# Retention, routed experts and channel mix on one core: the int64 narrowing's steps laid out one a call, with a third buffer for their results

## The chip, the core and the metric

The kernel runs on one core of a Trainium2 chip. The metric is the device time of one execution in microseconds (us); lower is better. The text names the engines as the profile does: PE (TensorE, matmuls), PEld (its weight loads), DVE (VectorE), ACT (ScalarE), POOL (GpSimd), SP (SyncE, which here only issues DMAs). Each engine works through its own instructions strictly in the order in which the program gives them. A piece of work waits for its inputs and for the buffer that it writes, and everything behind it on that engine waits as well.

## The reference

Three stages follow one another; the second and third are what the change touches.

```
B, H, S, D = 2, 8, 768, 64           # retention with decay, block by block -> out [B, H, S, D]
x = out.transpose(0, 2, 1, 3).reshape(2, 768, 512)

# experts: E = 8, F = 1024; every token goes to one expert e (argmax, or the one before, by a local gate)
h = np.maximum(x[b, s] @ w1[e], 0.0)           # w1 [8, 512, 1024]
out[b, s] = p[e] * (h @ w2[e])                 # w2 [8, 1024, 512]

# channel mix
xk = mu_k * x + (1.0 - mu_k) * x_prev;  xr = mu_r * x + (1.0 - mu_r) * x_prev
k = np.maximum(xk @ w_k, 0.0);  v = k * k @ w_v
r = 1.0 / (1.0 + np.exp(-(xr @ w_r)));  return r * v
```

The inputs `w_k` [512, 1024], `w_v` [1024, 512] and `w_r` [512, 512] of the last stage reach the kernel as 64-bit floats, viewed as int64, and have to be narrowed to 32 bits on the chip.

## The kernel before

**Matmuls by split values.** Every f32 operand is held as a high part (rounded for the fast matmul form) and a low part (the rest), and `split3` (L652) makes three matmuls of each product: high by high, high by low, low by high. Each weight therefore passes through `w_split` (L144): ACT copies a loaded piece of 128x1024 f32 to the high tile (L155), DVE subtracts to get the low one (L156), and a new load of a piece, four ahead, is put on SP's queue (L140, pool `stp`, 4 buffers `raw`). An expert has 8 such pieces, 4 of `w1` and 4 of `w2`.

**The expert loop** (L953). For each of 8 experts, `up` computes four pieces of h: 24 matmuls each into one of three PSUM buffers `ps_h`, then ACT makes `hh` (L669) and DVE makes `hl` (L670), which frees the buffer. `flip` transposes the next expert's inputs (PE L649) and splits them (ACT L173, DVE L174). `down` computes two pieces of y from the four `hh`/`hl`, 24 matmuls of 512 columns each. After expert 1's `up` and `flip`, `weights` (L807) computes softmax weights once: small DVE and ACT work.

**Side work.** After each piece of `up` (four times) and twice in each half of `down` (four times) the loop calls `side_w` (L932). The calls are counted through the kernel, c = 0 to 63; c mod 8 = 0 to 3 lie in `up`, 4 to 7 in `down`. A call does `ws` splits of weight pieces, then `ns` steps of the narrowing, then `vs` conversions of narrowed rows that stay on the chip (`divide`); the three numbers are set in L937 to L943. Splits run about one expert ahead of their use: the splits in `up(e)` are for the second weight of expert e + 1, those in `down(e)` for the first of expert e + 2.

**Narrowing** (`narrow`, L754) is a generator that goes on by one step each time `next(conv)` is called. After a first step that puts two reads of int64 pieces on SP's queue (`raw64`, 512 KB each, 2 buffers, L767), 20 pieces of 128x512 values follow, each in three steps:

- first step: `narrow_1` (L743, L744), two DVE instructions on t1, which holds the magnitude that ACT has made from the int64 piece (L739, `begin`);
- second step: `narrow_2` (L747, L748), which writes t2;
- third step: `narrow_3` (L751, L752), after which t2 holds the f32 values. The step then puts `begin` of the next piece on ACT (its magnitude) and the read of the piece after that on SP, which takes over the buffer just used up.

18 of the 20 results are written to DRAM from t2 (L788, 256 KB each), by SP in the call after; the last two stay in t2 until `divide`. The last 9 of the 73 weight pieces are loads of these written values, in calls 48 to 56. t1 and t2 are tags of the pool `tp` with 2 buffers each, and `mix_pair` (L889) uses the same tags in the channel mix.

Of the kernel before, what the change touches and what calls it, by code (L numbers as in the profile page):

```python
# [10 lines left out]
F32 = mybir.dt.float32  # L11
# [3 lines left out]
I32 = mybir.dt.int32  # L15
# [6 lines left out]
P = 128  # L22
# [22 lines left out]
def kernel(  # L45
# [84 lines left out]
    for kind, i, src, n, f in plan:  # L130
        m = PIECE // f
# [12 lines left out]
    def w_split(k=1, eng=dve):  # L144
        for _ in range(k):
            if at[1] >= len(pieces):
                return
            while at[0] <= at[1]:
                w_load()
            kind, i, src, n, f, j, m = pieces[at[1]]  # L150
            if (kind, i) not in W:
                W[kind, i] = w_tiles(kind, i, n, f)
            hi, lo = W[kind, i]
            t = staged.pop(at[1])
            act.copy(out=hi[:, j : j + m, :], in_=t)  # L155
            eng.tensor_tensor(out=lo[:, j : j + m, :], in0=t, in1=hi[:, j : j + m, :].bitcast(F32), op=ALU.subtract)  # L156
            at[1] += 1
            w_load()
# [469 lines left out]
    tp = ctx.enter_context(tc.tile_pool(name="tp", bufs=2))  # L628
# [4 lines left out]
    with ExitStack() as bctx:  # L633
# [104 lines left out]
        def magnitude(raw, t):  # L738
            act.activation(out=t.bitcast(F32), in_=words(raw)[2], func=AF.Abs)  # L739

        def narrow_1(t):

            dve.tensor_scalar(out=t.bitcast(F32), in0=t.bitcast(F32), scalar1=2.0**-15, scalar2=TOP64, op0=ALU.max, op1=ALU.min)  # L743
            dve.tensor_scalar(out=t, in0=t, scalar1=3, scalar2=0x3FFFFFFF, op0=ALU.logical_shift_left, op1=ALU.bitwise_and)  # L744

        def narrow_2(raw, t, t2, p2):
            dve.scalar_tensor_tensor(out=t2, in0=words(raw)[1], scalar=-(1 << 30), in1=t, op0=ALU.bitwise_and, op1=ALU.bitwise_or)  # L747
            dve.tensor_scalar(out=p2, in0=t2, scalar1=-(1 << 23), scalar2=None, op0=ALU.bitwise_and)  # L748

        def narrow_3(raw, p2, low, t2, x):  # L750
            dve.scalar_tensor_tensor(out=low, in0=words(raw)[0], scalar=2.0**-52, in1=p2, op0=ALU.mult, op1=ALU.mult)  # L751
            dve.tensor_tensor(out=x, in0=low, in1=t2.bitcast(F32), op=ALU.add)  # L752

        def narrow():  # L754

            n = DM
            parts = []
            for src, dst in ((wk, wk32), (wr, wr32), (wv, wv32)):
                sv, dv = (x.rearrange("p a b -> p (a b)") for x in (src, dst))
                parts += [(sv[:, j : j + n], dv[:, j : j + n]) for j in range(0, dv.shape[1], n)]  # L760
            parts += [(wv[:, j, :], j) for j in range(NV, NF)]
            raws, ts = {}, {}

            def read(k):
                if k < len(parts):
                    raws[k] = bp.tile([P, n], mybir.dt.int64, name=f"raw64_{k}", tag="raw64")
                    sp.dma_start(out=raws[k], in_=parts[k][0])  # L767

            def begin(k):
                if k < len(parts):  # L770
                    ts[k] = tp.tile([P, n], I32, name="t1", tag="t1")
                    magnitude(raws[k], ts[k])

            read(0)
            read(1)
            yield
            begin(0)
            for k in range(len(parts)):
                t2 = tp.tile([P, n], I32, name="t2", tag="t2")
                narrow_1(ts[k])  # L780
                yield
                narrow_2(raws[k], ts[k], t2, ts[k])
                yield
                narrow_3(raws[k], ts[k].bitcast(F32), ts[k].bitcast(F32), t2, t2.bitcast(F32))
                if isinstance(parts[k][1], int):
                    whole.append((parts[k][1], t2.bitcast(F32)))
                else:
                    written.append(lambda t=t2, k=k: sp.dma_start(out=parts[k][1], in_=t.bitcast(F32)))  # L788
                begin(k + 1)
                read(k + 2)  # L790
                yield
# [3 lines left out]
        def divide():  # L795

            j, x = whole.pop(0)
            hi, lo = (w[:, j, :] for w in W["w2", NE])
            act.copy(out=hi, in_=x)
            dve.tensor_tensor(out=lo, in0=x, in1=hi.bitcast(F32), op=ALU.subtract)  # L800

        conv = narrow()
        perm = bp.tile([P, 2, 2 * P], F32R, name="perm", bufs=1)
        ylast = []
# [83 lines left out]

        def mix_pair(i, a, hi, lo, old, new, quick=False):  # L889

            t, m = (tp.tile([P, 2, 2 * P], F32, name=x, tag=x) for x in ("t1", "t2"))
            r = slice(2 * a, 2 * a + 2)

            def older(j):
                x, m1 = old(j), mus1[:, i, 2 * a + j : 2 * a + j + 1]
                o = t[:, j, 2 * P - x.shape[-1] :]
                if not j and x.shape[-1] < 2 * P:
                    (dve if quick else pool).memset(t[:, :, 0:1], 0.0)
                if quick:
                    dve.tensor_scalar(out=o, in0=x, scalar1=m1, scalar2=None, op0=ALU.mult)  # L900
                else:
                    act.activation(out=o, in_=x, func=AF.Copy, scale=m1)

            def newer(j):
                d = 2 * a + j
                dve.scalar_tensor_tensor(out=m[:, j, :], in0=new(j), scalar=mus[:, i, d : d + 1], in1=t[:, j, :], op0=ALU.mult, op1=ALU.add)
                if quick:
                    act.copy(out=hi[:, d, :], in_=m[:, j, :])

            for f in (older, newer):  # L910
                for j in range(2):
                    f(j)
            if not quick:
                act.copy(out=hi[:, r, :], in_=m)
            dve.tensor_tensor(out=lo[:, r, :], in0=m, in1=hi[:, r, :].bitcast(F32), op=ALU.subtract)

        def mix_first(a, i=0):
            if not a:
                x0[i] = mix_tiles(i, 0)
            mix_pair(i, a, *x0[i], lambda j: px[1 + a][:, j, 0 : 2 * P - 1], lambda j: px[1 + a][:, j, :], not i)  # L920
# [11 lines left out]
        def side_w():  # L932
            c = calls[0]
            calls[0] += 1
            late = list(written)

            ws, ns, vs = 1, 1, 0  # L937
            if c < 4:
                ws, ns = (2, 2, 1, 1)[c], c == 2
            elif c < 24:  # L940
                ns = 2 if c % 8 in (4, 6) or c in (5, 7, 13, 15) else 1
            elif c >= 52:
                ws, ns, vs = ((1, 2, 0), (1, 0, 0), (1, 0, 0), (1, 0, 0), (1, 0, 0), (1, 0, 1), (1, 0, 0), (0, 0, 1), (1, 0, 0), (1, 0, 0), (0, 0, 0), (0, 0, 0))[c - 52]  # L943
            w_split(ws)
            for _ in range(ns):
                next(conv, None)
            for _ in range(vs):
                divide()
            for w in late:
                w()  # L950
            del written[: len(late)]

        for e in range(NE):  # L953
            up(e, side_w)
            if e + 1 < NE:
                flip(e + 1)
            if e + 2 < NE:
                gather(e + 2, gidx, NT)
            if e == 1:
                weights()  # L960
            if e == 3:
                weights_by_slot()
            down(e, side_w)
# [3 lines left out]
    with ExitStack() as mctx:  # L967
# [48 lines left out]
        def mix(n, i):  # L1016
            if n >= NN:
                return None
            x = mix_tiles(i, n)
            for a in range(2):  # L1020
                mix_pair(i, a, *x, lambda j: xt[n][:, 2 * a + j, 0:GS], lambda j: xt[n][:, 2 * a + j, 1 : 1 + GS])
            return x
# [164 lines left out]
```

## Time and profile before

| what | us |
|---|---|
| median of 3 runs | 474.19 (473.14 to 475.46) |
| profiled execution, its own time | 471.66 |
| its span on the core | 470.0 |
| PE busy in the span | 441.2 (94%) |
| DVE busy | 311.1 (66%) |
| ACT busy | 229.2 (49%) |
| 80 to 156 us (experts 0 to 2): PE busy | 59.3 of 76 |
| 156 to 277 us (experts 2 to 7): PE busy | 120.8 of 121 |

The profile shows one execution. In a timeline each row has a start, the busy time of the instructions in it, and in brackets the time that the engine was idle before it and what it waited for. Starts of instructions that follow one another without a wait give the pace; the busy time of one is longer than that pace, since the end of one lies over the start of the next. "PEclk" is the granted clock of PE as a share of full speed, 2.4 GHz; 0.50 is its lower level, 1.2 GHz.

### The profile page before, as it was taken

Reading aid. Unit: us, or ns where it says so; the run is one execution under the profiler, and the core shown is the slowest. Engines: PE = TensorE matmul, PEld = TensorE weight load, DVE = VectorE, ACT = ScalarE, POOL = GpSimd, SP = SyncE. Lnnn points to the kernel's source line nnn. Section 1 sums busy time; section 2 is a strip of 40 time slices with the busy share of each in tenths; the row PEclk is TensorE's granted clock in tenths of the full one; section 3 lists DMA queues with packets and bytes.
Section 4 is the critical chain, followed back from the end, with each engine's and each line's share of the span. In section 5 each row is a group of like instructions: output and inputs, shape, how many; then the busy total and the mean of one; then the engine's idle time right before and its main releaser. Section 6 shows DMA issues by size and latency. Waiting matters only on the chain.

```text
span 470.0 us, 8309 instructions
## 1 busy us (share of the span) xinstructions
PE 441.2 (94%) x3243; PEld 394.1 (84%) x3243; DVE 311.1 (66%) x602; ACT 229.2 (49%) x386; POOL 67.2 (14%) x92
## 2 busy tenths in 40 slices
PE   7999988997595799999999999999999999999996
PEld 6878876977585689898989899989898998989886
DVE  6578775767887898999998775655436253361501
ACT  2455523553663456565656463676446264563410
POOL 3432223501201103142300200100000000000000
PEclk9999999999799799999999999999999999999999
DMA  7899944697768889999988640300202002000011
GB/s 240 301 377 326 376 180 135 215 329 250 248 246 276 262 267 339 306 342 354 355 296 300 209 155 22 113 2 1 91 1 67 24 0 91 0 24 23 1 45 46
DMA packets 29111, 85.03 MB, mean 181 GB/s; under 512 B 4351, under 2 KB 5131, under 8 KB 29068
## 3 DMA queue, kind: packets, MB, share of 16 engines
q1 hardware_dynamic: 25004, 73.45, 46.2%
q0 software_dynamic: 2624, 8.39, 4.9%
q10 hardware_dynamic: 1440, 2.62, 1.5%
q8 instruction: 26, 0.43, 0.3%
q14 instruction: 17, 0.14, 0.1%
HBM read 68.71 MB, written 15.74 MB: 180 GB/s over the span
## 4 chain that ended last, share of the span: by engine, by line
PE 62%; DVE 8%; DMA 7%; ACT 4%; issue 1%; SPq 0%; DVEq 0%; ACTq 0%
PE ps_y L657 5%; PE ps_y L655 5%; PE ps_y L656 5%; PE ps_v L655 5%; PE ps_v L656 5%; PE ps_v L657 5%; PE ps_h L655 5%; PE ps_h L656 4%; PE ps_h L657 4%; PE ps_k L1028 4%; PE ps_k L1029 4%; PE ps_k L1035 4%; DMA raw<-in_wk_dram 3%; DMA wk<-t 3%; PE ps_r L656 2%; PE ps_r L655 2%
## 5 line engine op out<-in xcount | busy, mean ns | idle before, releaser
L655 PE MATMUL ps_h<-xsTh,w1h 128*128 128x256 f32 x256 | 74.4, 291 | 16.4 <-DVE hl L670 16.4
L656 PE MATMUL ps_h<-xsTl,w1h 128*128 128x256 f32 x256 | 74.0, 289 | 0.1
L657 PE MATMUL ps_h<-xsTh,w1l 128*128 128x256 f32 x256 | 73.6, 287 | 0.0
L655 PEld LDWEIGHTS ps_h<-xsTh,w1h 128*128 128x128 f32 x256 | 50.3, 197 | 17.6 <-DVE hl L670 16.8
L1067 DVE TENSOR_TENSOR sq<-rl 128x512 f32<-128x512 f32 x24 | 16.6, 691 | 55.9 <-ACT rl L1064 55.9
L655 PE MATMUL ps_y<-w2h,hh 128*128 128x512 f32 (+1 forms) x136 | 52.6, 387 | 0.0
L657 PE MATMUL ps_y<-w2h,hl 128*128 128x512 f32 (+1 forms) x136 | 52.1, 383 | 0.0
L656 PE MATMUL ps_y<-w2l,hh 128*128 128x512 f32 (+1 forms) x136 | 51.9, 382 | 0.0
L656 PEld LDWEIGHTS ps_h<-xsTl,w1h 128*128 128x128 f32 x256 | 50.3, 197 | 0.9 <-DVE xsTl L174 0.5
L657 PEld LDWEIGHTS ps_h<-xsTh,w1l 128*128 128x128 f32 x256 | 50.2, 196 | 0.0
L156 DVE TENSOR_TENSOR w1l<-raw,w1h 128x1024 fp32r<-128x1024 f32 x38 | 46.0, 1216 | 6.3 <-ACT w1h L155 6.3
L156 DVE TENSOR_TENSOR w2l<-raw,w2h 128x1024 fp32r<-128x1024 f32 x35 | 42.7, 1220 | 5.8 <-ACT w2h L155 5.2
L155 ACT CAST w1h<-raw 128x1024 fp32r<-128x1024 f32 x38 | 38.9, 1052 | 4.9 <-DMA raw<-in_w_dram 4.9
L726 POOL DMA_INDIRECT Y_n<-y,sidx x16 | 18.5, 1157 | 153.2 <-ACT y L716 108.4
L655 PE MATMUL ps_v<-w2h,k2h 128*128 128x512 f32 (+1 forms) x104 | 39.2, 377 | 0.0
L656 PE MATMUL ps_v<-w2l,k2h 128*128 128x512 f32 (+1 forms) x104 | 38.8, 373 | 0.0
L657 PE MATMUL ps_v<-w2h,k2l 128*128 128x512 f32 (+1 forms) x104 | 38.8, 373 | 0.0
L155 ACT CAST w2h<-raw 128x1024 fp32r<-128x1024 f32 x35 | 36.6, 1045 | 3.7 <-DMA raw<-in_w_dram 3.7
L739 ACT ACTIVATE t<-raw 128x512 f32<-128x512 f32 x20 | 13.5, 673 | 48.7 <-DMA raw<-in_wk_dram 24.8
L669 ACT ACTIVATE hh<-ps_h 128x512 fp32r<-128x512 f32 x32 | 19.1, 596 | 24.9 <-PE ps_h L657 24.9
L657 PEld LDWEIGHTS ps_y<-w2h,hl 128*128 128x128 f32 x136 | 25.6, 188 | 6.1 <-DVE hl L670 0.8
L656 PEld LDWEIGHTS ps_y<-w2l,hh 128*128 128x128 f32 x136 | 25.6, 188 | 5.1
(210 smaller groups left out, 975.7 us busy)
## 6 DMA issues: line engine op xcount, KB each, us to landing
raw<-in_w_dram SPq DMA_DIRECT2D x64, 512.0 KB
kv<-in_kv_dram SPq DMA_DIRECT2D x12, 512.0 KB
qk<-in_qk_dram SPq DMA_DIRECT2D x11, 512.0 KB
raw<-in_wk_dram SPq DMA_DIRECT2D x8, 512.0 KB
raw<-in_wv_dram SPq DMA_DIRECT2D x8, 512.0 KB
out_dram<-o SPq DMA_DIRECT2D x11, 256.0 KB
X_n<-xn ACTq DMA_DIRECT2D x10, 256.0 KB
xg<-Y_n SPq DMA_DIRECT2D x10, 256.0 KB
```

What stands on the lines that cost most here:

```text
L155: act.copy(out=hi[:, j : j + m, :], in_=t)
L156: eng.tensor_tensor(out=lo[:, j : j + m, :], in0=t, in1=hi[:, j : j + m, :].bitcast(F32), op=ALU.subtract)
L655: pe.matmul(ps, wh, xh, start=first, stop=False)
L656: pe.matmul(ps, wh, xl, start=False, stop=False)
L657: pe.matmul(ps, wl, xh, start=False, stop=last)
L669: act.activation(out=hh, in_=ps, func=AF.Relu)
L726: pool.indirect_dma_start(out=Y_n[:, :], out_offset=bass.IndirectOffsetOnAxis(ap=sidx[:, t, e : e + 1], axis=0), in_=y, in_offset=None)
L739: act.activation(out=t.bitcast(F32), in_=words(raw)[2], func=AF.Abs)
L1028: pe.matmul(ps[:, j, :], wkh[:, d, f], x[0][:, d, :], start=j == d == 0, stop=False, skip_group_check=True)
L1029: pe.matmul(ps[:, j, :], wkl[:, d, f], x[0][:, d, :], start=False, stop=False, skip_group_check=True)
L1035: pe.matmul(ps[:, j, :], wkh[:, d, f], x[1][:, d, :], start=False, stop=d == ND - 1, skip_group_check=True)
L1067: dve.tensor_tensor(out=sq, in0=rl, in1=rl, op=ALU.mult)
```

## The change

The whole difference:

```
--- before.py
+++ after.py
@@ -776,7 +776,7 @@
             yield
             begin(0)
             for k in range(len(parts)):
-                t2 = tp.tile([P, n], I32, name="t2", tag="t2")
+                t2 = tp.tile([P, n], I32, name="t2", tag="t2", bufs=3)
                 narrow_1(ts[k])
                 yield
                 narrow_2(raws[k], ts[k], t2, ts[k])
@@ -888,7 +888,7 @@
 
         def mix_pair(i, a, hi, lo, old, new, quick=False):
 
-            t, m = (tp.tile([P, 2, 2 * P], F32, name=x, tag=x) for x in ("t1", "t2"))
+            t, m = (tp.tile([P, 2, 2 * P], F32, name=x, tag=x, bufs=k) for x, k in (("t1", 2), ("t2", 3)))
             r = slice(2 * a, 2 * a + 2)
 
             def older(j):
@@ -937,10 +937,10 @@
             ws, ns, vs = 1, 1, 0
             if c < 4:
                 ws, ns = (2, 2, 1, 1)[c], c == 2
-            elif c < 24:
-                ns = 2 if c % 8 in (4, 6) or c in (5, 7, 13, 15) else 1
             elif c >= 52:
-                ws, ns, vs = ((1, 2, 0), (1, 0, 0), (1, 0, 0), (1, 0, 0), (1, 0, 0), (1, 0, 1), (1, 0, 0), (0, 0, 1), (1, 0, 0), (1, 0, 0), (0, 0, 0), (0, 0, 0))[c - 52]
+                ws, ns, vs = ((1, 2, 0), (1, 2, 0), (1, 2, 0), (1, 0, 0), (1, 0, 0), (1, 0, 1), (1, 0, 0), (0, 0, 1), (1, 0, 0), (1, 0, 0), (0, 0, 0), (0, 0, 0))[c - 52]
+            elif c % 8 == 5:
+                ns = 2
             w_split(ws)
             for _ in range(ns):
                 next(conv, None)
```

The tag t2 gets 3 buffers. The steps of the narrowing are given out in another way: before, calls 4 to 7 took two each, calls 8 to 11 one, calls 12 to 15 two, calls 16 to 23 one or two (10 in 8 calls), calls 24 to 51 one each, and call 52 the last two. Now calls 4 to 51 take one each, with a second one where c mod 8 is 5, which is nine steps (three pieces) an expert, and calls 52, 53 and 54 take two each. There are 61 steps in both. In expert 0's `down` eight steps become five; in expert 1 twelve become nine; in expert 2 ten become nine; in experts 3, 4 and 5 eight become nine; in expert 6 six become ten.

First place: DVE, from the second-to-last weight piece that is split in expert 0's `down` up to the first `hl` of expert 1. `t` is t1 or t2, `raw_1` and `raw_2` are int64 pieces, `raw` with a four-digit number alone a weight piece. Before:

```order
L156 TENSOR_TENSOR w1l_1567<-raw_1495,w1h_1566 128x1024
L747 SCALAR_TENSOR_TENSOR t_1601<-raw_1_1499,t_1597 128x512
L748 TENSOR_SCALAR t_1597<-t_1601 128x512
L751 SCALAR_TENSOR_TENSOR t_1597<-raw_1_1499,t_1597 128x512
L752 TENSOR_TENSOR t_1601<-t_1597,t_1601 128x512
L156 TENSOR_TENSOR w1l_1567<-raw_1532,w1h_1566 128x1024
L743 TENSOR_SCALAR t_1628<-t_1628 128x512
L744 TENSOR_SCALAR t_1628<-t_1628 128x512
L747 SCALAR_TENSOR_TENSOR t_1649<-raw_2_1599,t_1628 128x512
L748 TENSOR_SCALAR t_1628<-t_1649 128x512
L670 SCALAR_TENSOR_TENSOR hl_0_1683<-ps_h_0_1657,hh_0_1682 128x512
```

And now:

```order
L156 TENSOR_TENSOR w1l_1567<-raw_1495,w1h_1566 128x1024
L743 TENSOR_SCALAR t_1597<-t_1597 128x512
L744 TENSOR_SCALAR t_1597<-t_1597 128x512
L156 TENSOR_TENSOR w1l_1567<-raw_1532,w1h_1566 128x1024
L747 SCALAR_TENSOR_TENSOR t_1621<-raw_1_1499,t_1597 128x512
L748 TENSOR_SCALAR t_1597<-t_1621 128x512
L670 SCALAR_TENSOR_TENSOR hl_0_1671<-ps_h_0_1645,hh_0_1670 128x512
```

Between the two weight splits and `hl_0` the third step of piece 1 and both steps of piece 2 are gone; they come after `hl_0`.

Second place: ACT, over the same stretch, from the cast of the same weight piece to `hh_1` of expert 1 (L739 is the magnitude, L716 a copy of y). Before:

```order
L155 CAST w1h_1566<-raw_1495 128x1024
L739 ACTIVATE t_1628<-raw_2_1599 128x512
L155 CAST w1h_1566<-raw_1532 128x1024
L716 COPY y_1_1655<-ps_y_1_1606 128x512
L669 ACTIVATE hh_0_1682<-ps_h_0_1657 128x512
L155 CAST w2h_1686<-raw_1570 128x1024
L739 ACTIVATE t_1694<-raw_3_1630 128x512
L669 ACTIVATE hh_1_1724<-ps_h_1_1699 128x512
```

And now:

```order
L155 CAST w1h_1566<-raw_1495 128x1024
L155 CAST w1h_1566<-raw_1532 128x1024
L716 COPY y_1_1643<-ps_y_1_1603 128x512
L669 ACTIVATE hh_0_1670<-ps_h_0_1645 128x512
L155 CAST w2h_1674<-raw_1570 128x1024
L739 ACTIVATE t_1682<-raw_2_1599 128x512
L669 ACTIVATE hh_1_1712<-ps_h_1_1687 128x512
```

The magnitude of piece 2 stood ahead of a cast, a copy and `hh_0`; it now stands behind them, and that of piece 3 is no longer in the stretch.

Third place: DVE, the end of expert 1's `down`, up to the first `hl` of expert 2. Before:

```order
L156 TENSOR_TENSOR w1l_1854<-raw_1767,w1h_1853 128x1024
L747 SCALAR_TENSOR_TENSOR t_1887<-raw_5_1808,t_1883 128x512
L748 TENSOR_SCALAR t_1883<-t_1887 128x512
L751 SCALAR_TENSOR_TENSOR t_1883<-raw_5_1808,t_1883 128x512
L752 TENSOR_TENSOR t_1887<-t_1883,t_1887 128x512
L156 TENSOR_TENSOR w1l_1854<-raw_1802,w1h_1853 128x1024
L743 TENSOR_SCALAR t_1914<-t_1914 128x512
L744 TENSOR_SCALAR t_1914<-t_1914 128x512
L747 SCALAR_TENSOR_TENSOR t_1935<-raw_6_1885,t_1914 128x512
L748 TENSOR_SCALAR t_1914<-t_1935 128x512
L670 SCALAR_TENSOR_TENSOR hl_0_1969<-ps_h_0_1943,hh_0_1968 128x512
```

And now:

```order
L156 TENSOR_TENSOR w1l_1842<-raw_1755,w1h_1841 128x1024
L743 TENSOR_SCALAR t_1871<-t_1871 128x512
L744 TENSOR_SCALAR t_1871<-t_1871 128x512
L156 TENSOR_TENSOR w1l_1842<-raw_1790,w1h_1841 128x1024
L747 SCALAR_TENSOR_TENSOR t_1895<-raw_4_1796,t_1871 128x512
L748 TENSOR_SCALAR t_1871<-t_1895 128x512
L670 SCALAR_TENSOR_TENSOR hl_0_1945<-ps_h_0_1919,hh_0_1944 128x512
```

Here two of the four last steps before `hl_0` have moved behind it or into later calls (eight DVE instructions of narrowing become four, with two weight splits in both).

## Rows read from the trace of the kernel before

**Rows 1.** waits, longest first: engine line waited for, us in total, times, longest
```profile
PE ps_h L655 <- DVE hl L670: 16.4, 2, 8.5
...
DVE t L747 <- DMA wk<-t: 3.0, 2, 2.3
```

**Rows 2.** timeline of PE, 111 to 163 us: start, busy us, [idle before]
```profile
111.66 0.28 PE L655 MATMUL ps_h<-xsTh,w1h 128*128 128x256 f32 x1
...
114.42 0.28 PE L657 MATMUL ps_h<-xsTh,w1l 128*128 128x256 f32 x1
...
122.61 0.58 PE L655 MATMUL ps_h<-xsTh,w1h 128*128 128x256 f32 x1 [7.92 <-DVE hl L670]
...
126.86 1.04 PE L649 MATMUL ps_x<-ident,xs 128*128 128x128 f32 x8
...
156.22 0.58 PE L655 MATMUL ps_h<-xsTh,w1h 128*128 128x256 f32 x1 [8.51 <-DVE hl L670]
...
160.71 1.04 PE L649 MATMUL ps_x<-ident,xs 128*128 128x128 f32 x8
```

**Rows 3.** windows: stretch, its length, busy time of each engine, PEclk, DMA share, GB/s
```profile
8.00:12.00 4.00, 3.20 (x44) 3.00 (x41) 3.33 (x10) 0.53 (x1) 1.04 (x1) 0.68 1.00 318
...
72.00:76.00 4.00, 2.60 (x19) 1.66 (x18) 2.88 (x10) 2.05 (x4) 2.36 (x4) 1.00 0.70 243
...
120.00:123.00 3.00, 0.39 (x2) 0.39 (x3) 2.22 (x5) 2.89 (x5) 2.18 (x3) 0.50 0.83 211
```

**Rows 4.** timeline of ACT, 116 to 149 us
```profile
116.41 0.66 ACT L739 ACTIVATE t<-raw 128x512 f32<-128x512 f32 x1 [6.95 <-DMA raw<-in_wk_dram]
...
118.38 0.60 ACT L669 ACTIVATE hh<-ps_h 128x512 fp32r<-128x512 f32 x1
...
132.31 0.67 ACT L739 ACTIVATE t<-raw 128x512 f32<-128x512 f32 x1 [3.66 <-DMA raw<-in_wk_dram]
...
148.50 0.66 ACT L739 ACTIVATE t<-raw 128x512 f32<-128x512 f32 x1 [7.34 <-DMA raw<-in_wk_dram]
```

**Rows 5.** timeline of DVE, 107 to 122 us
```profile
107.46 0.69 DVE L747 SCALAR_TENSOR_TENSOR t<-raw,t 128x512 int32<-128x512 int32 x1
...
108.54 1.22 DVE L156 TENSOR_TENSOR w1l<-raw,w1h 128x1024 fp32r<-128x1024 f32 x1
...
109.67 0.68 DVE L751 SCALAR_TENSOR_TENSOR t<-raw,t 128x512 f32<-128x512 uint32 x1
...
111.00 0.42 DVE L743 TENSOR_SCALAR t<-t 128x512 f32<-128x512 f32 x1
...
121.87 0.68 DVE L670 SCALAR_TENSOR_TENSOR hl<-ps_h,hh 128x512 fp32r<-128x512 f32 x1
```

**Rows 6.** timeline of DVE, 134 to 203 us
```profile
134.69 0.25 DVE L811 TENSOR_TENSOR ex<-lg,mx 128x96 f32<-128x96 f32 x1
...
138.07 1.22 DVE L156 TENSOR_TENSOR w1l<-raw,w1h 128x1024 fp32r<-128x1024 f32 x1
...
166.92 1.28 DVE L174 TENSOR_TENSOR xsTl<-ps_x,xsTh 128x512 fp32r<-128x512 f32 x2
...
180.79 0.69 DVE L670 SCALAR_TENSOR_TENSOR hl<-ps_h,hh 128x512 fp32r<-128x512 f32 x1 [0.91 <-ACT hh L669]
...
202.05 0.67 DVE L670 SCALAR_TENSOR_TENSOR hl<-ps_h,hh 128x512 fp32r<-128x512 f32 x1
```

**Rows 7.** chain that ended last, in order of time: the transposes of two flips
```profile
232.13 0.87 PE ps_x L649 x8
...
255.70 0.87 PE ps_x L649 x8
```

**Rows 8.** timeline of SP, 110 to 144 us: the reads of raw64
```profile
110.38 0.33 SPq L767 DMA_DIRECT2D raw<-in_wk_dram  x1
...
124.32 0.33 SPq L767 DMA_DIRECT2D raw<-in_wk_dram  x1
...
143.05 0.33 SPq L767 DMA_DIRECT2D raw<-in_wk_dram  x1
```

More of the change, by code (lines that the diff above doesn't have):

```diff
@@ L778, in narrow @@
             for k in range(len(parts)):
-                t2 = tp.tile([P, n], I32, name="t2", tag="t2")
+                t2 = tp.tile([P, n], I32, name="t2", tag="t2", bufs=3)
                 narrow_1(ts[k])
@@ L889, in mix_pair @@
         def mix_pair(i, a, hi, lo, old, new, quick=False):
-            t, m = (tp.tile([P, 2, 2 * P], F32, name=x, tag=x) for x in ("t1", "t2"))
+            t, m = (tp.tile([P, 2, 2 * P], F32, name=x, tag=x, bufs=k) for x, k in (("t1", 2), ("t2", 3)))
             r = slice(2 * a, 2 * a + 2)
@@ L939, in side_w @@
                 ws, ns = (2, 2, 1, 1)[c], c == 2
-            elif c < 24:
-                ns = 2 if c % 8 in (4, 6) or c in (5, 7, 13, 15) else 1
             elif c >= 52:
-                ws, ns, vs = ((1, 2, 0), (1, 0, 0), (1, 0, 0), (1, 0, 0), (1, 0, 0), (1, 0, 1), (1, 0, 0), (0, 0, 1), (1, 0, 0), (1, 0, 0), (0, 0, 0), (0, 0, 0))[c - 52]
+                ws, ns, vs = ((1, 2, 0), (1, 2, 0), (1, 2, 0), (1, 0, 0), (1, 0, 0), (1, 0, 1), (1, 0, 0), (0, 0, 1), (1, 0, 0), (1, 0, 0), (0, 0, 0), (0, 0, 0))[c - 52]
+            elif c % 8 == 5:
+                ns = 2
             w_split(ws)
```

## The prediction

> **What bounds the kernel now.** I read the page's slices first: PE is full nearly everywhere from 156 us on, and thin between 108 and 156. The list of waits says why. Nearly all idle time of PE between 80 us and the end of the experts is one wait that occurs twice, 16.4 us for `hl` (L670) [rows 1]: `up` has three PSUM buffers, and its fourth piece cannot begin before DVE has emptied the first. The timeline of PE shows both places, expert 1 (7.92 us idle, so from 114.69) and expert 2 (8.51 us), each time ahead of the fourth piece [rows 2]. After them the granted clock is 0.50, that is 1.2 GHz, in the window read [rows 3], so that piece runs slowly as well. At full clock its 24 matmuls have a pitch of (114.42 - 111.66) / 23 = 0.12, 2.88 us in all; here they take 126.86 - 122.61 = 4.25 and 160.71 - 156.22 = 4.49 [rows 2]. Both places together cost 7.92 + 8.51 + 1.37 + 1.61 = 19.4 us.
>
> `hl` is late because it stands on DVE behind side work of the calls before it. In expert 0's `down` that is four weight splits and eight narrowing steps; in expert 1's, the same. Those steps wait in turn: ACT's magnitude of piece 2 sat 6.95 us until its int64 read had landed, with a weight cast and `hh` queued behind it [rows 4], and twice DVE waited for the write out of t2, 3.0 us in all [rows 1].
>
> **Part 1, fewer steps ahead of `hl` of expert 1.** I lay out DVE from 107.46, when the first step of piece 0 is over and the next cast is done; up to there the order is that of before. The paces, start to start [rows 5]: second step 108.54 - 107.46 = 1.08, weight split 1.13, third step 111.00 - 109.67 = 1.33; a first step is two instructions of 0.42, 0.84. Now the row up to `hl` is split, second, third, split, first, split, second: 3 x 1.13 + 2 x 1.08 + 1.33 + 0.84 = 7.72, so `hl` starts at 115.18 instead of 121.87. PE followed `hl`'s start by 122.61 - 121.87 = 0.74, so it goes on at 115.92: 1.2 us of idle time are left of 7.92. ACT is not late for this: the magnitude that waited until 116.41 now stands behind `hh` of the first piece, and only `hh` of the second piece and what follows waits for it; DVE comes to that one after a split and a third step, at about 118.3.
>
> **Part 2, the same in expert 2.** From `hl` of one expert to `hl` of the next, DVE took 202.05 - 180.79 = 21.26 with eight steps and hardly a wait [rows 6]. Nine steps (one third step more) make 22.59. Expert 1 also has the softmax weights, 138.07 - 134.69 = 3.38 [rows 6]. So `hl` of expert 2 starts at 115.18 + 22.59 + 3.38 = 141.15, PE goes on at 141.89. PE's own period is 255.70 - 232.13 = 23.57 [rows 7], so it wants to go on at 115.92 + 23.57 = 139.49: 2.4 us of idle time are left of 8.51.
>
> **Part 3, the other experts.** From here DVE runs about as late as PE allows and needs 22.59 of PE's 23.57 us an expert, so nothing more is lost as long as its own waits stay under 0.98 us an expert. One place is tight. Of the three reads an expert, the one issued at c mod 8 = 3 is wanted two calls later. From the start of L751 in that call, DVE has a third step, the flip's two subtractions (1.28 in the row [rows 6]), two splits, a first, a second and a third step: 1.33 + 1.28 + 2.26 + 0.84 + 1.08 + 1.33 = 8.12 until the next split. That split needs the read issued (110.38 - 109.67 = 0.71 [rows 5, 8]), landed (L), and three ACT operations (magnitude, cast, copy: 118.38 - 116.41 = 1.97 [rows 4]). DVE therefore waits L - 5.44. L is not shown for the new order; I take it from issue to the start of a magnitude that waited for it. There are 13 such pairs after the first; the shortest is 148.50 - 143.05 = 5.45, the longest 132.31 - 124.32 = 7.99 [rows 4, 8], their mean 6.4. I take the mean, because the bytes an expert lie between those of the stretches in which these reads were made. DVE then waits 1.0 an expert, as much as it has. Expert 6 has ten steps, so its block is about 1.1 longer and PE pays that; for scatter of L I add 0.4. With L always at 7.99 five experts would pay 22.59 + 2.55 - 23.57 = 1.57 each, 7.9 in all, and the 1.1; at the short end nothing.
>
> **Part 4, the rest.** The third t2 buffer takes away the two waits of 3.0 us [rows 1]; these lay inside the late `hl`, and I don't count them twice. The written results are the same 18, only later: the last write now stands on SP just before the loads of its neighbours, calls 52 to 54, which splits use four calls on and PE only in the last stage; that stage covers a write that lands in 6 us several times over, so nothing. t1 keeps two buffers, and the magnitude that fills one comes after the third step that frees it, as before. `mix_pair` in the last stage also gets the third buffer; no wait on t2 shows there, so nothing. What stands ahead of call 4, and PE's order throughout, stay the same.
>
> **Sum.** 19.4 gone; 1.2 + 2.4 + 1.1 + 0.4 = 5.1 left or new: 14.3 us off. On the profiled execution that is 471.66 - 14.3 = 457.4. The median of the runs is 2.5 above that execution, so against 474.19 I forecast 459.9.
>
> **Rivals.**
>
> *Reads that land late.* As in part 3 with L at its long end: 1.2 + 2.4 + 7.9 + 1.1 = 12.6 left, 6.8 gained: 467.4; halfway, 464. For it: the narrowing's traffic is now spread over stretches that also load weights. Against it: 7.99 is the longest of 13.
>
> *The clock falls at short waits too.* It was 0.68 in the window 8 to 12 us, where PE was busy for 3.20 of 4 us, and 1.00 in 72 to 76, where it was busy for only 2.60 [rows 3]; so the rows speak both ways. If PE lost its clock at the waits of 1.2 and 2.4, two pieces would again cost about 1.5 each: 462.9. If it did so in each of seven experts, 10.5: 470.4. The Trainium skill, "TensorE: Matmul & The Clock Gate", section "A second HAM failure mode: psum-queue depth-cycling", speaks for this: it tells of a kernel whose PE paused shortly between groups as it cycled through PSUM buffers, and whose clock went up and down for it. By that rule the time would be near 470 if PE paused in every expert; the trace's short pauses in 72 to 76 us did not do it.
>
> *DVE not at the deadline at all.* If waits that I laid out on paper overlap better, all 19.4 may go: 454.8.
>
> *Slower.* One mechanism: the reads fall so far behind that DVE waits for two of the three an expert. The read issued at c mod 8 = 0 has 9.96 us of DVE work before it is missed (three `hl` of 0.68, three splits, two third steps, a first, a second) and is missed from L = 8.1; from there each us of L costs 2 an expert. The gain is used up when five experts pay (19.4 - 4.7) / 5 = 2.9 each, at L = 8.7, and the kernel is slower by over 0.5% from L = 8.9. At 9.2 it would be 479. Against it: no L in the trace is over 7.99.
>
> *It does not do what it says.* SP could reach the reads so late, behind a weight load that waits for its buffer, that `hl` is held up as before: 474. The first read that matters is issued after the same third step as before, at about 110.4, so this is unlikely.
>
> **Chances.** The forecast (457 to 462.5) 50%, late reads 20%, clock 13%, everything gone 8%, slower 5%, no effect 4%. The range 456 to 467 leaves out the two last, the far ends of late reads and clock, and half of the best case. A measurement of this kernel can tell about 0.5% from no change; faster by more than that 91%, within it 5%, slower 4%.
>
> **What would show it.** Right: PE's wait for `hl` falls from 16.4 us to about 4 to 6, its two largest pieces in experts 1 and 2 are near 1.2 and 2.4, no DVE wait for a write of t2 is left, and the granted clock stays at 1.00 (2.4 GHz) from 16 us on. Wrong: new waits of PE in experts 3 to 7 with DVE waiting for ACT and ACT for int64 reads (late reads); windows at 0.50 after waits of some 2 us (clock); or a gain that is lost again after 280 us, where I expect the same lengths as before.

## The result, and the profile after

| | before | after |
|---|---|---|
| median of 4 runs each, us | 474.28 | 457.34 (456.0 to 461.21) |
| profiled execution, its own time | 471.66 | 458.06 |
| its span | 470.0 | 456.4 |

The ratio is 0.9656, 95% interval [0.9591, 0.9721]: about 17 us off by the medians, 13.6 by the two profiled executions. In a later set of runs the same kernel had 458.81 against 472.25, 0.9711 [0.9688, 0.9733]. The profiled execution after is one of the four runs and lies 0.7 above their median; the one before lies below all of its runs. The forecast was 459.9, from 456 to 467, so the medians beat it by 2.6 us and the profiled execution (457.4 forecast) fell short of it by 0.7.

The list of waits after the change (engine, what waited, what for: us in total, times, longest), whose last line answers to the first of [rows 1]:

```profile
ACT t L739 <- DMA raw<-in_wk_dram: 24.4, 7, 6.0
...
DVE t L743 <- ACT t L739: 5.1, 1, 5.1
DVE w1l L156 <- ACT w1h L155: 4.9, 5, 1.8
...
PE ps_h L655 <- DVE hl L670: 4.4, 2, 2.5
```

PE's wait for `hl` has gone from 16.4 to 4.4 us, and a DVE wait on the write out of t2 (the second of [rows 1]) occurs no more. The timeline of PE after (start, busy us, operation, idle before in brackets) shows the two places that [rows 2] show, and the start of the last stage, which before began with the same matmul at 312.98:

```profile
117.30 0.39 PE L655 MATMUL ps_h<-xsTh,w1h 128*128 128x256 f32 x1 [2.50 <-DVE hl L670]
...
120.28 1.03 PE L649 MATMUL ps_x<-ident,xs 128*128 128x128 f32 x8
...
143.09 0.39 PE L655 MATMUL ps_h<-xsTh,w1h 128*128 128x256 f32 x1 [1.94 <-DVE hl L670]
...
147.57 1.04 PE L649 MATMUL ps_x<-ident,xs 128*128 128x128 f32 x8
...
299.39 0.39 PE L1028 MATMUL ps_k<-w1h,w1h 128*128 128x256 f32 x1 [0.52 <-ACT w1h L914]
```

The last stage starts 312.98 - 299.39 = 13.59 us sooner and takes 157.0 us in both (470.0 - 312.98, 456.4 - 299.39): all of the gain is made in the experts and nothing is given back. The windows (stretch, length, busy us of PE, PEld, DVE, ACT, POOL, then PEclk, DMA share, GB/s) show where the clock fell. Before, it was low around both waits, in expert 1 [rows 3] and in expert 2:

```profile
158.00:159.00 1.00, 1.00 (x7) 1.00 (x6) 1.00 (x2) 0.00 (x0) 0.00 (x0) 0.50 0.56 131
```

After, it falls once in the experts, behind the wait in expert 2, and once ahead of them, at 76 us, where it stood at 1.00 before:

```profile
76.00:77.00 1.00, 1.00 (x6) 0.70 (x5) 1.00 (x3) 0.00 (x0) 0.00 (x0) 0.50 0.00 0
...
115.00:118.00 3.00, 0.70 (x5) 0.70 (x6) 2.96 (x5) 1.63 (x3) 1.88 (x2) 1.00 0.99 334
118.00:121.00 3.00, 3.00 (x28) 3.00 (x27) 2.96 (x5) 2.46 (x4) 2.24 (x2) 1.00 0.90 323
...
144.00:145.00 1.00, 1.00 (x7) 1.00 (x6) 0.97 (x3) 1.00 (x3) 0.89 (x1) 0.50 0.97 354
145.00:146.00 1.00, 1.00 (x7) 1.00 (x7) 1.00 (x2) 1.00 (x2) 0.69 (x2) 0.50 0.86 346
...
147.00:148.00 1.00, 1.00 (x9) 1.00 (x8) 0.96 (x3) 0.48 (x2) 0.00 (x0) 0.81 0.83 291
```

After the wait of 2.50 us in expert 1 it stayed at 1.00 (2.4 GHz); after the shorter one in expert 2 it went to 0.50 (1.2 GHz), and the piece behind took 147.57 - 143.09 = 4.48 us. The same piece at full clock takes 120.28 - 117.30 = 2.98 in expert 1, so that cost 1.5.

The gain can be followed along PE's rows [rows 2]: `flip` starts 126.86 - 120.28 = 6.58 us sooner in expert 1, 160.71 - 147.57 = 13.14 us sooner in expert 2, and the last stage 13.59 us sooner. So nearly all of it lies at the two places; the last 0.45, gained in experts 3 to 7, is not traced.

DVE after, in place of [rows 5, 6]: the start of the row of work ahead of `hl`, the first `hl` of experts 1 to 3, and the waits for casts in experts 3 to 5:

```profile
107.83 0.43 DVE L743 TENSOR_SCALAR t<-t 128x512 f32<-128x512 f32 x1 [5.05 <-ACT t L739]
...
108.78 1.23 DVE L156 TENSOR_TENSOR w1l<-raw,w1h 128x1024 fp32r<-128x1024 f32 x1
...
116.57 0.68 DVE L670 SCALAR_TENSOR_TENSOR hl<-ps_h,hh 128x512 fp32r<-128x512 f32 x1
...
142.35 0.68 DVE L670 SCALAR_TENSOR_TENSOR hl<-ps_h,hh 128x512 fp32r<-128x512 f32 x1
...
166.15 0.69 DVE L670 SCALAR_TENSOR_TENSOR hl<-ps_h,hh 128x512 fp32r<-128x512 f32 x1
...
185.26 1.23 DVE L156 TENSOR_TENSOR w1l<-raw,w1h 128x1024 fp32r<-128x1024 f32 x1 [0.56 <-ACT w1h L155]
...
208.97 1.23 DVE L156 TENSOR_TENSOR w1l<-raw,w1h 128x1024 fp32r<-128x1024 f32 x1 [1.26 <-ACT w1h L155]
...
233.24 1.22 DVE L156 TENSOR_TENSOR w1l<-raw,w1h 128x1024 fp32r<-128x1024 f32 x1 [1.81 <-ACT w1h L155]
```

From the row's first split to `hl` it is 116.57 - 108.78 = 7.79, as laid out (7.72). But the row starts at 108.78 and not at 107.46, because the first int64 value came later. SP's issue of that read and ACT's magnitude that waited for it, before and after:

```profile
99.16 0.80 SPq L767 DMA_DIRECT2D raw<-in_wk_dram  x2
...
105.84 0.67 ACT L739 ACTIVATE t<-raw 128x512 f32<-128x512 f32 x1 [4.78 <-DMA raw<-in_wk_dram]
```

```profile
99.04 0.80 SPq L767 DMA_DIRECT2D raw<-in_wk_dram  x2
...
107.13 0.67 ACT L739 ACTIVATE t<-raw 128x512 f32<-128x512 f32 x1 [6.02 <-DMA raw<-in_wk_dram]
```

6.68 us before, 8.09 after, with nothing changed ahead of it in the program. In the second execution of the changed kernel it was 7.05, so the difference between 6.68 and 8.09 is scatter as far as these three show.

### The profile page after: what moved, and what is told of

It is laid out like the page before. It is cut to its first block, busy times and chain, and to the rows that moved or that the text cites. A ratio compares the mean times of both kernels' runs of the same rounds, so it can differ in the third digit from the quotient of the medians.

```text
span 456.4 us, 8308 instructions
## 1 busy us (share of the span) xinstructions
PE 436.7 (96%) x3243; PEld 391.3 (86%) x3243; DVE 309.9 (68%) x602; ACT 229.2 (50%) x386; POOL 65.6 (14%) x92
## 4 chain that ended last, share of the span: by engine, by line
PE 69%; DVE 13%; DMA 8%; ACT 4%; issue 4%; POOL 1%; SPq 1%; DVEq 0%; ACTq 0%; POOLq 0%
PE ps_y L655 5%; PE ps_y L657 5%; PE ps_y L656 5%; PE ps_v L655 5%; PE ps_v L656 5%; PE ps_v L657 5%; PE ps_h L655 5%; PE ps_h L656 5%; PE ps_h L657 5%; PE ps_k L1028 4%; PE ps_k L1029 4%; PE ps_k L1035 4%; DMA raw<-in_w_dram 4%; DVE w1l L156 2%; PE ps_r L655 2%
## 5 line engine op out<-in xcount | busy, mean ns | idle before, releaser
L657 PE MATMUL ps_h<-xsTh,w1l 128*128 128x256 f32 x256 | 73.0, 285 | 0.0
L657 PE MATMUL ps_y<-w2h,hl 128*128 128x512 f32 (+1 forms) x136 | 51.9, 382 | 0.0
L657 PEld LDWEIGHTS ps_h<-xsTh,w1l 128*128 128x128 f32 x256 | 49.8, 195 | 0.0
L739 ACT ACTIVATE t<-raw 128x512 f32<-128x512 f32 x20 | 13.5, 677 | 55.8 <-DMA raw<-in_wk_dram 24.4
L657 PE MATMUL ps_v<-w2h,k2l 128*128 128x512 f32 (+1 forms) x104 | 38.8, 373 | 0.0
L657 PEld LDWEIGHTS ps_y<-w2h,hl 128*128 128x128 f32 x136 | 25.6, 188 | 5.5 <-DVE hl L670 0.2
L655 PEld LDWEIGHTS ps_y<-w2h,hh 128*128 128x128 f32 x136 | 25.6, 188 | 5.1
```

The lines of the kernel that those rows point to most:

```text
L655: pe.matmul(ps, wh, xh, start=first, stop=False)
L657: pe.matmul(ps, wl, xh, start=False, stop=last)
```

## The experiments

The theory: `hl` of experts 1 and 2 was late because of the narrowing steps ahead of it on DVE, and the new order of the steps is the gain; the third buffer adds nothing. The rivals: the buffer is the gain (it takes away the 3.0 us of [rows 1]); the reads set the time; or DVE's work as such does.

**One part alone.** The spread steps with two t2 buffers (excerpt; `mix_pair` goes back in the same way):

```
-                t2 = tp.tile([P, n], I32, name="t2", tag="t2", bufs=3)
+                t2 = tp.tile([P, n], I32, name="t2", tag="t2")
```

> The even spread with two t2 buffers, as in the kernel before. My theory: the time goes with the number of steps that stand ahead of the first hl of experts 1 and 2, and the third buffer is not needed for it. In the changed kernel the second step of piece k + 2 comes 7.0 to 9.9 us after the write of piece k is issued, and a write landed in 5.5 to 6.4 us, so at most a wait of a few tenths: PE waits for hl 4 to 6 us, 457 to 458.5. Rival (the third buffer carries part of the gain): DVE waits for the write of t2 again, 2 to 3 us as before, 460 or more.

Measured: 459.93 against 472.62, 0.9706 [0.9652, 0.9761], an interval that overlaps the changed kernel's two (0.9656 and 0.9711). The time is 1.4 above the expected range and close to the rival's 460, but the rival's mechanism is absent: DVE waited for no write. PE waited 1.32 and 2.67 us in experts 1 and 2, and 0.50 and 1.23 in experts 6 and 7. Within the scatter, the third buffer isn't needed.

The old order of the steps with three buffers (excerpt, as edited from the changed kernel; calls 52 to 54 go back as well):

```
+            elif c < 24:
+                ns = 2 if c % 8 in (4, 6) or c in (5, 7, 13, 15) else 1
-            elif c % 8 == 5:
-                ns = 2
```

> The old handing out of steps with three t2 buffers. My theory: DVE's two waits for the write of t2 (0.74 and 2.26 us) go and nothing else, because the magnitude of piece 2 still waits for its read ahead of hh: PE still waits about 13.4 us for hl, and the piece behind each wait still runs at the lower clock; 470 to 472. Rival (the buffer is the main part): PE waits under 9 us, 466 or less.

Measured: 472.01 against 472.62, 0.9971 [0.9941, 1.0001]. PE's timeline there:

```profile
123.98 0.58 PE L655 MATMUL ps_h<-xsTh,w1h 128*128 128x256 f32 x1 [7.97 <-DVE hl L670]
...
129.27 1.28 PE L649 MATMUL ps_x<-ident,xs 128*128 128x128 f32 x8
...
155.08 0.58 PE L655 MATMUL ps_h<-xsTh,w1h 128*128 128x256 f32 x1 [4.70 <-DVE hl L670]
...
160.37 1.10 PE L649 MATMUL ps_x<-ident,xs 128*128 128x128 f32 x8
```

The buffer takes 3 us off PE's waits (13.4 in all, with 0.72 in expert 3, as expected), but the time shows only 0.6 us of it (0 to 2.8 by the interval), and expert 1 waits as long as ever. In this execution the two slow pieces took 5.29 us each and not 4.25 and 4.49, which takes 1.8 of the 3 back, and PE was 1.55 us later than in the kernel before when expert 1's inputs were flipped (95.22 against 93.67). The steps are the gain.

**Where the ninth step stands.** The second step of a call at c mod 8 = 1, in `up`, and not at 5:

```
-            elif c % 8 == 5:
+            elif c % 8 == 1 and c > 1:
```

> The changed kernel with the second step of an expert's nine in the call c mod 8 = 1 (in up) instead of 5 (in down). One step fewer stands ahead of the first hl of an expert and one more ahead of its third and fourth. Theory (all DVE work up to each hl counts, and the fourth hl, which down needs, has about 1 us less to spare): PE's wait for the first hl of expert 1 falls by about 1.1 us and about as much comes back as waits of down for the later hl: within 1 us of the changed kernel, 456.3 to 458.3. Rival (only the steps ahead of the first hl count): 1.1 off, and 1.6 more if the clock no longer falls in expert 2: 454.6 to 456.2.

Measured: 460.56, 0.9721 [0.9662, 0.9779], a miss, 2.3 us above what was expected. PE's timeline:

```profile
117.06 0.38 PE L655 MATMUL ps_h<-xsTh,w1h 128*128 128x256 f32 x1 [1.19 <-DVE hl L670]
...
126.52 0.50 PE L657 MATMUL ps_y<-w2h,hl 128*128 128x512 f32 x1 [0.79 <-DVE hl L670]
...
144.20 0.39 PE L655 MATMUL ps_h<-xsTh,w1h 128*128 128x256 f32 x1 [2.26 <-DVE hl L670]
```

Ahead of the fourth piece of `up` the two waits add up to 3.45 us, against 4.44 and 3.79 in the changed kernel's two executions (2.50 + 1.94 and 1.40 + 2.39), and PE now also waits for a later `hl`, in `down` (L657), three times, 2.2 us in all. Moving this one step put a wait elsewhere on DVE's row and took less than that away.

**Expert 0 alone.** Its `down` has five steps as now, while calls 8 to 23 keep the old order (excerpt; calls 52 to 54 take 2, 2 and 1).

```
+            elif c < 8:
+                ns = 2 if c == 5 else 1
+            elif c < 24:
+                ns = 2 if c % 8 in (4, 6) or c in (13, 15) else 1
```

> The steps are thinned in expert 0's down only (5 instead of 8), as in the changed kernel; calls 8 to 51 are handed out as in the kernel before, and calls 52 to 54 take what is left (2, 2, 1); three t2 buffers. Theory (each expert's lateness is made by the steps ahead of its own first hl): PE's wait in expert 1 falls to about 2 us with no lower clock behind it, 7 us gained; expert 2 keeps a wait of 6 to 9 us, 465 to 469. Rival (what is put off in expert 0 is paid in expert 2, since 12 steps with late reads still have to be done ahead of it): PE's wait there grows to 12 or more, 470 to 474.

Measured: 469.03 against 473.78, 0.9884 [0.9803, 0.9964]. No wait of PE for `hl` in expert 1 and the whole lateness in expert 2:

```profile
152.23 0.58 PE L655 MATMUL ps_h<-xsTh,w1h 128*128 128x256 f32 x1 [9.13 <-DVE hl L670]
```

Time and wait lie just at the upper end of what was expected, below the rival's. So expert 2's wait comes from expert 1's own twelve steps, with the waits on reads that stand among them (DVE stood 3.67 us ahead of a split at 148.36, behind a magnitude that had waited for its read). Thinning expert 0 alone is not enough; thinning expert 1 alone was not run. (When expert 1's inputs were flipped, at 97.17, PE was 3.2 us later in this execution than in the changed kernel's, 94.00, which is why expert 1 shows no wait at all.)

**DVE's work up and down.** First without the clamp of the narrowing (L743), 20 instructions at a pace of 0.46 us, 9.2 in all; what this leaves out stands in the expectation.

> The changed kernel without the clamp (L743), the first of the six DVE instructions of each narrowed piece; tiny magnitudes are then not kept from wrapping, nothing else is left out. It takes 0.46 us off DVE for each of 20 pieces, 9.2 in all. Theory (DVE is what PE waits for in experts 1 and 2, and then about level with PE): two clamps fewer ahead of the first hl of expert 1 (0.9), five ahead of that of expert 2 (2.3): PE's waits of 4.4 us fall to about 2, and with luck the lower clock (1.6) goes; 2 to 4 off, 453.5 to 455.5. Rival (DVE is the limit through all experts): up to 9 off, 449 or less. Second rival (nothing of DVE's work counts any more): same, 457.

Measured: 456.61, 0.9632 [0.9551, 0.9714], 1.1 above the expected range and so by its median next to the second rival; the profiled execution, the fastest of the four, has a span of 453.1, and PE waited 0.94 and 1.54 us. DVE's waits for casts in experts 3 to 5 grew to 1.72, 1.95 and 2.19 us: part of the work taken away came back as waits for ACT. Then the clamp twice:

> The changed kernel with the clamp (L743) done twice, which changes no value: 0.46 us more of DVE work a piece, 9.2 in all, 1.4 an expert. Theory (DVE's block of 22.6 us and about 1 us of waits stands right under PE's 23.57): each further us counts almost in full from expert 1 on; PE's waits for hl rise from 4.4 to 10 to 13 us, spread over all experts, 463.5 to 466.5. Rival (past expert 2 PE has room to spare): only the 2.3 us ahead of expert 2's hl count, 459 to 460.5.

Measured: 464.79, 0.9805 [0.9716, 0.9893]. Two rows of PE's timeline, the longest wait and one of three that the changed kernel doesn't have:

```profile
145.15 0.58 PE L655 MATMUL ps_h<-xsTh,w1h 128*128 128x256 f32 x1 [3.11 <-DVE hl L670]
...
268.46 0.39 PE L655 MATMUL ps_h<-xsTh,w1h 128*128 128x256 f32 x1 [0.94 <-DVE hl L670]
```

Neither edit moved the time by the whole 9.2 us. Beside the changed kernel's first numbers, less work gave 1 us by the medians and 3 by the profiles, and more work cost 7 and 6; beside its second (458.81, span 457.4), less gave 2 and 4, and more cost 6 and 5. More work cost more than less work gave, but the intervals are too wide to give the difference a size. The total of PE's waits in the second (6.8 for `up`, 0.5 for `down`) is below the 10 to 13 that I had written down, though the time was as expected: that hit is in part luck, since 1.2 of the 5.9 us between the spans were there when expert 1's inputs were flipped (95.22 against 94.00), and 1.8 were not traced.

**The reads.** First, the first two pieces read at call 1 and not 2:

```
-                ws, ns = (2, 2, 1, 1)[c], c == 2
+                ws, ns = (2, 2, 1, 1)[c], c == 1
```

> The changed kernel with the first two int64 reads issued one call sooner (call 1, not 2). In the changed kernel DVE stands idle for 5.05 us ahead of the first narrowing step, until the first read has landed (8.1 us after its issue). Theory: DVE starts 2.5 to 4 us sooner, so the first hl of experts 1 and 2 come that much sooner; PE's 4.4 us of waits fall to under 1 and the lower clock in expert 2 (1.6) goes too; 452.5 to 455. Rival (the transfers are the limit there: the reads only push back the weight loads behind them, so casts and splits come later by as much): 456.5 to 459.

Measured: 456.97, 0.9626 [0.9588, 0.9665]: a miss, 2 us above the upper end and inside the rival's range. The profiled execution is the slowest of the six (460.09) and says little on the start. DVE's wait for the first value fell from 5.05 to 2.35 and PE did not wait in expert 1, but PE was 3.7 us later than in the changed kernel when expert 1's inputs were flipped (94.00 there), and DVE's first step came no sooner (107.83 there):

```profile
97.71 0.98 PE L649 MATMUL ps_x<-ident,xs 128*128 128x128 f32 x7 [1.79 <-DMA xs<-X_n,gidx]
```

```profile
108.08 0.43 DVE L743 TENSOR_SCALAR t<-t 128x512 f32<-128x512 f32 x1 [2.35 <-ACT t L739]
```

PE waited 2.25 in expert 2 and its clock fell there, and DVE waited further on, in experts 3 to 5, after the last of which PE waited 0.29 in expert 6:

```profile
186.40 1.23 DVE L156 TENSOR_TENSOR w1l<-raw,w1h 128x1024 fp32r<-128x1024 f32 x1 [1.40 <-ACT y L716]
...
210.75 1.23 DVE L156 TENSOR_TENSOR w1l<-raw,w1h 128x1024 fp32r<-128x1024 f32 x1 [1.88 <-ACT w1h L155]
...
235.88 1.23 DVE L156 TENSOR_TENSOR w1l<-raw,w1h 128x1024 fp32r<-128x1024 f32 x1 [1.73 <-ACT w1h L155]
```

Second, all reads one step ahead, with a third buffer for what is read (and two for t2 and y to make room; excerpt):

```
+                    raws[k] = bp.tile([P, n], mybir.dt.int64, name=f"raw64_{k}", tag="raw64", bufs=3)
+            read(2)
-                read(k + 2)
+                read(k + 3)
```

> The changed kernel with three buffers for the int64 pieces, so that each read is issued one piece (about 8 us) sooner; the room is taken from t2 (2 buffers) and from y (2 instead of 3). In the changed kernel DVE waits 0.6, 1.3 and 1.8 us in experts 3, 4 and 5 for a cast that stands behind a magnitude whose read is late, but PE does not wait there. Theory: these DVE waits go, PE's waits in experts 1 and 2 (4.4 us) hardly change, 456 to 458.5. Rival (the late reads hold the whole row of DVE work, so they cost PE): 2 us or more off, 453 to 455.

Measured: 458.43, 0.9643 [0.956, 0.9727], no different from the changed kernel, and as expected. PE waited 1.90 and 1.96 us in experts 1 and 2, and DVE in experts 3 to 5 no longer for a cast behind a read. Neither was run beside the changed kernel on the same chip. Last, both together, and beside it the changed kernel again on the same chip:

> The first two pieces of expert 1 are read at call 1 of expert 0 as in the run that read sooner, and every other piece a step further ahead as in the run that read ahead (three buffers for the values read; two for narrowed values and for y). If the late reads were what kept the earlier start from paying (DVE's waits of 1.40, 1.88 and 1.73 us in experts 3 to 5 of that run), both gains add up: no wait of PE in expert 1, one of 1 to 2.3 in expert 2, no later one, no DVE wait for the splitting's ScalarE step in experts 3 to 5, and 452.5 to 455 us, below the changed kernel beside it by 2 to 4. If instead DVE's own work is the limit from expert 2 on (rival), the time lies where the others lie, 456 to 458.5, within 1.5 us of the changed kernel, and PE waits again for hl in experts 4 to 6 although no read is late.

> The changed kernel once more, beside the run that joins both changes of the reads, as what that one is compared with on the same chip: 456 to 459 us, PE's waits for hl of 2.0 to 3.0 us in expert 1 and 1.5 to 2.5 in expert 2. Whether the clock falls to half after the wait in expert 2, as in its first profile, is open: if a wait of about 2 us always does it, it falls again; if it depends on more than the wait's length, it may stay at 1.00.

Measured: 454.67 (453.8 to 457.14, 6 runs) for both, 0.9638 [0.961, 0.9665], and 458.81 (458.38 to 459.12, 5 runs) for the changed kernel. The ranges don't touch: 4.1 us, and the lowest median here. By the ratio to the kernel before, the joined version (0.9638), the sooner read (0.9626) and the reads ahead (0.9643) can't be told apart, so these runs don't show that both edits are needed. In the groups by line (busy, mean ns, then idle before and its releasers), the magnitudes' waits for the int64 reads, of the changed kernel first, of the joined version second:

```profile
L739 ACT ACTIVATE t<-raw 128x512 f32<-128x512 f32 x20 | 13.7, 683 | 57.6 <-DMA raw<-in_wk_dram 25.4 <-DMA raw<-in_wv_dram 19.3 <-DMA raw<-in_wr_dram 7.7
```

```profile
L739 ACT ACTIVATE t<-raw 128x512 f32<-128x512 f32 x20 | 13.5, 676 | 4.5 <-DMA raw<-in_wk_dram 4.5
```

PE and DVE of the changed kernel in that set of runs:

```profile
116.82 0.39 PE L655 MATMUL ps_h<-xsTh,w1h 128*128 128x256 f32 x1 [1.40 <-DVE hl L670]
...
143.05 0.39 PE L655 MATMUL ps_h<-xsTh,w1h 128*128 128x256 f32 x1 [2.39 <-DVE hl L670]
...
239.75 0.38 PE L655 MATMUL ps_h<-xsTh,w1h 128*128 128x256 f32 x1 [0.56 <-issue]
```

```profile
234.88 1.23 DVE L156 TENSOR_TENSOR w1l<-raw,w1h 128x1024 fp32r<-128x1024 f32 x1 [2.71 <-ACT w1h L155]
...
239.01 0.69 DVE L670 SCALAR_TENSOR_TENSOR hl<-ps_h,hh 128x512 fp32r<-128x512 f32 x1
```

And of the joined version:

```profile
115.18 0.39 PE L655 MATMUL ps_h<-xsTh,w1h 128*128 128x256 f32 x1 [0.26 <-DVE hl L670]
...
141.00 0.39 PE L655 MATMUL ps_h<-xsTh,w1h 128*128 128x256 f32 x1 [1.99 <-DVE hl L670]
...
143.97 1.04 PE L649 MATMUL ps_x<-ident,xs 128*128 128x128 f32 x8
```

```profile
140.27 0.67 DVE L670 SCALAR_TENSOR_TENSOR hl<-ps_h,hh 128x512 fp32r<-128x512 f32 x1
...
162.64 0.67 DVE L670 SCALAR_TENSOR_TENSOR hl<-ps_h,hh 128x512 fp32r<-128x512 f32 x1
...
185.08 0.68 DVE L670 SCALAR_TENSOR_TENSOR hl<-ps_h,hh 128x512 fp32r<-128x512 f32 x1
```

Two things are to be read here. The wait labelled "issue" at 239.75 is one for `hl`: that `hl` ended at 239.70, and it was late by the 2.71 us that DVE had waited for a cast behind a read. And with no read late, DVE's block is 185.08 - 162.64 = 22.44 us, the 22.59 of part 2, against PE's 23.57 [rows 7]. Of the spans' difference (457.4 - 452.8 = 4.6) the rows account for 0.5 (expert 1's inputs flipped at 94.13 and not 94.62, behind a wait for gathered rows), 1.1 and 0.4 of shorter waits, 1.5 of clock (4.47 against 2.97 for the piece) and the 0.56: 4.1. The 0.5 left are not traced. The 1.5 of clock is not shown to be the edit's: of the changed kernel's five runs, the one with a mean clock of 0.999 took 458.76, no less than the four with 0.993 (458.38 to 459.12). The changed kernel's wait of 1.40 in expert 1 lies below the 2.0 to 3.0 expected.

## Why the prediction was right, and where it was off

**What bounds the kernel: right.** The one wait fell from 16.4 to 4.4, the time by 13.6 in the profiled executions, and the two halves of the edit apart show that the steps' order did it.

**Part 1: the length right, the start wrong.** 7.79 for 7.72; but 2.50 us were left and not 1.2. The step that failed is "I lay out DVE from 107.46": it took the time of one execution over, since nothing in the order changes up to there. What stands there is a wait for a read, whose landing went from 6.68 to 8.09. That put DVE's row back by 1.3 us, the whole difference. The read that comes a call sooner made the wait 0 and 0.26 in its two runs, the 0 in an execution whose PE was 3.7 us late.

**Part 2: right.** 142.35 - 116.57 = 25.78 for 25.97, and 1.94 left for 2.4.

**Part 3: the place right, the cost about right and hidden once.** DVE waits at the split named (c mod 8 = 6), 0.56, 1.26 and 1.81 us in three experts, against 1.0 forecast. Its five blocks from 142.35 to 261.38 are 23.81 us each, 0.24 more than PE's 23.57. In the first profile that cost PE nothing. The rows fit this reason: the slow piece in expert 2 had put PE back by 1.5 and so gave DVE that much room. Where PE had not been put back (two t2 buffers), 0.50 and 1.23 appeared in experts 6 and 7, about the 1.1 + 0.4 that the sum carried. In the second execution of the changed kernel PE had been put back as well, but DVE's waits were longer (1.65, 1.18, 1.23 and 2.71 in experts 2 to 5), and 0.56 appeared.

**Part 4: right.** With two t2 buffers the time is the same within the intervals, and the last stage has the same length.

**The sum** had 14.3 off; it was 13.6 in the profile and 13.4 by the medians of the last set of runs (472.25 - 458.81), 16.9 by those of the first. Three terms were mis-sized and one was not in it: 1.3 more in expert 1, 0.4 less in expert 2, 1.5 less in the later experts, and 1.5 for the clock, which was to stay at 1.00. They nearly cancel, so the closeness of the total is in part luck. The last step, 2.5 more for the median than for the profiled execution, did not carry over either: after the change the median was 0.7 less than the profiled one, and with that the forecast was 2.6 too high. The full-clock piece of 2.88 was 0.1 short: from its first matmul to `flip` it takes 2.97 or 2.98. In *Slower*, the instructions named add up to 10.01 and not 9.96, and its 8.1 is not worked out from them; the forecast uses neither.

**The rivals.** *Late reads* held in small. I looked for them in experts 3 to 7 and bounded them with 467; they cost most at the first read, and about 0.5 later. That they also stood between this kernel and 454.67 I had not seen. That this is near "everything gone" (454.8) is chance: in its set of runs it is 17.6 off and not 19.4, and expert 2's 1.99 is still there. *The clock* fell at one of its two places and cost 1.5, half of what that rival (462.9) put on top of the forecast. What I held against it, the short pauses in 72 to 76 us without a fall, was one execution's luck: the changed kernel's clock fell right there (last section). *Slower* and *no effect* are out; the first needed landings of 8.9 us in five experts, and one such was seen.

**The misses among the experiments.** Four times lay above their ranges: two buffers by 1.4, the step in `up` by 2.3, less work by 1.1, the sooner read by 2.0. All four were set from 457.34; the changed kernel's later median was 458.81, so more than 1 us of each may be scatter between sets. For the sooner read there is a reason to be argued and not shown: I counted what the start gains and not that DVE, once PE is ahead by it, has no room left for its waits on reads.

## What to carry to other kernels

When an engine's side work is to be spread, count the instructions between two deadlines of that engine and hold them against the period of the engine that waits: nine steps (22.4 us) fit into 23.57, twelve did not, and the one move of a single step that was tried only moved the wait. What is then left is the slack's size (1 us an expert here), and every late read is paid from it, so look at the reads together with the work: both edits of the reads together gave 4 us beside the changed kernel, and what each gives alone was not measured beside it. In a forecast, don't take over the start of a chain that begins behind a DMA from one execution: give it the scatter of that landing. And before you read one profile against another, compare them at a point that the edit can't reach: behind its second pause for rows ahead of expert 0, PE went on at 74.78 in the changed kernel and at 78.26 in the sooner read.

## What was not expected of the hardware

**The clock at waits of about 2 us.** Ahead of the fourth piece in expert 2, PE waited 1.5 to 3.1 us in nine of the executions with the spread steps. The clock fell to 0.50 after 1.94 (changed kernel), 1.96 (reads ahead), 2.25 (sooner read), 2.39 (changed, second time) and 3.11 (more work), and stayed at 1.00 after 1.54 (less work), 1.99 (both reads), 2.26 (step in `up`) and 2.67 (two buffers). In expert 1 it stayed at 1.00 after 2.50, 1.90, 1.77, 1.40, 1.32, 1.19 and 0.94. So the length of the wait alone doesn't decide; what else does stays open. Where it fell, the piece took 4.25 to 4.48 us for 2.97. At about 76 us, ahead of every edit, PE pauses twice for rows from DRAM, 0.5 to 1.3 us each. In seven of all twelve executions the clock fell within 2 us behind the second pause, in the changed kernel's two as well, and in the kernel before it did not. With a fall PE took 18.4 to 18.5 us from the second pause to its next wait for rows, without one 17.66. The Trainium skill, "TensorE: Matmul & The Clock Gate", section "A second HAM failure mode: psum-queue depth-cycling", describes a clock that goes up and down when PE pauses shortly and often between groups of matmuls. The traces here show a single pause of about 2 us ahead of the fall, five times of these nine, and no going up and down from one group to the next.

**A read of 512 KB** (128 rows of 512 int64) took 4.55 to 8.97 us in the changed kernel's first profile from SP's issue to the ACT instruction that waited for it, 8.97 for the one issued at 144.86; the trace of before had shown 5.45 to 7.99 [rows 4, 8]. The program's order up to the first read was the same in both kernels, and its landing still differed by 1.4 us.
